# Sixteen low-bit steps of the weight conversion written for GpSimd, and a range check ordered behind the last ELU

## The chip, the cores and the metric

The kernel runs on one core of a Trainium2 chip. In this text PE is TensorE (matmuls; PEld is its weight load), DVE is VectorE, ACT is ScalarE, POOL is GpSimd, and SP is SyncE, which here only issues DMAs. The metric is the device time of one execution in microseconds. Before the change three runs gave 660.2, 660.67 and 663.14 us; their median, 660.67 us, is the time before.

## The reference, cut to what matters

The reference is a windowed attention with a few sink keys, and behind it a two-layer network with an ELU between its layers.

```python
# q, k, v: (4, 8, 768, 64) float32; n_sink = 4, window = 128
scores = q @ k^T / 8, kept where key < n_sink or 0 <= query - key < window
a = softmax(scores)
x = (a @ v), heads put side by side: 3072 tokens x 512
h = x @ w_in                        # 512 x 2048, weights arrive as float64
g = where(h > 0, h, exp(min(h, 0)) - 1)
out = (g @ w_out)                   # 2048 x 512, float32
```

The two weight matrices are products of a float32 array and a float64 scalar and reach the kernel as 64-bit words, two 32-bit words to an element.

## The kernel before, in words

The 3072 tokens are cut into nine chunks: three of 256 tokens, six of 384. For every chunk the attention is computed for four pairs of heads (scores on PE at L540/541, or L547 for the first two chunks; range reduction on DVE at L566; exponentials on ACT at L568; the probabilities are split in a high and a low 16-bit part, by ACT at L580 and DVE at L581; a transposing DMA on SP at L599 brings them into the layout of the second matmul; PE multiplies by the values at L610 and L615; ACT L623 and DVE L624 write the chunk's `x`). The feed-forward of a chunk then runs over 16 slices of the hidden width: 12 matmuls into `h` (L651), the ELU in three steps (ACT L659, DVE L661 and L662), the split of the result in `gh` (ACT L664) and `gl` (POOL L665), and 6 or 9 matmuls into the output accumulators (L672). The first two chunks are done in halves, so that only 16 of the 32 weight pieces are wanted at first.

The weights come in 32 pieces of 128 x 512 elements, piece 2f of `w_in` and 2f+1 of `w_out`. `weights(k)` makes a piece usable: a DMA of 512 KB brings the 64-bit words into `raw` (L395). Then `weight_f32` builds a 32-bit float of each: step 0 on ACT (L267) scales the high word into a PSUM tile, `acc`; step 1 on DVE (L268) takes the three top bits of the low word; step 2 on DVE (L269) takes the sign; step 3 on DVE (L270) shifts the float by three bits and puts the four together in `wv`. ACT (L416) rounds `wv` to a 16-bit `w`, and POOL (L417) writes what is left as a second 16-bit part. Steps 1 and 2 write alternating 16-bit halves of one of two buffers `wu`; six buffers `raw` hold what the DMA brought.

A planner at trace time sets the order in which each engine gets its instructions. Every piece of work is a task with an engine, an assumed duration, and the tasks it depends on; PE's order is given by positions, and for the other engines a list schedule with due times, worked backward from PE's order, decides. `keep_order` then forces that order on each engine's in-order queue. An assumed duration has no other effect than on that order.

At the end the kernel decides whether the numbers stayed in a range in which the fast path holds. `in_range` (DVE, L725 to L731, eight small operations) gathers maxima, a one-column matmul (L741) sums over partitions, `decide` (DVE L735 to L737) multiplies the verdict into a flag, and L967 writes it as an integer. All five engines load that integer (L968) and branch over the slow path (L969). In the planner's order `in_range` depends on the last exponentials (`exps_done`), not on the last DVE step of the ELU.

Of the kernel before, what the change touches and what calls it, by code (L numbers as in the profile page):

```python
# [16 lines left out]
ALU = mybir.AluOpType  # L17
# [28 lines left out]
LAG = 2  # L46
WHOLE = 2
DUP = 2
AHEAD = 5
V_AT = 7  # L50
V_AT0 = 5.0
RINGS = dict(kqs=2, kq=3, vs=2, vm=1, vhl=2, e=3, st=6, pq=3, pt=6, g=2, gh=3, x=7, wv=4, s=2, po=1, h=2, wu=2, sv=2, wps=1, raw=6)
# [40 lines left out]
class Plan:  # L93
# [7 lines left out]
    def add(self, eng, dur, fn, *args, deps=(), lat=0.0, pos=None, or_=None):  # L101

        t = Task(eng, dur, fn, args, deps, lat, pos)
        if or_:
            t.ways[or_[0]] = or_[1:]
        self.tasks.append(t)
        return t

    def ring(self, name, writers, users):

        r = self.rings.setdefault(name, [])
        r.append((writers, users))
# [128 lines left out]
def act_us(n, scaled=False):  # L241
    return 0.17 + 0.00088 * n + (0.08 if scaled else 0.0)
# [13 lines left out]

def weight_f32(nc, v, d, u, raw):

    ui = u.bitcast(U16).rearrange("p (f t) -> p f t", t=2)
    words = raw.rearrange("p (f t) -> p f t", t=2)
    halves = raw.bitcast(U16).rearrange("p (f t) -> p f t", t=4)
    return (
        lambda: nc.scalar.activation(d, words[:, :, 1].bitcast(F32), AF.Copy, scale=2.0**-111),  # L267
        lambda: nc.vector.tensor_scalar(ui[:, :, 0], halves[:, :, 1], 13, None, ALU.logical_shift_right),  # L268
        lambda: nc.vector.tensor_scalar(ui[:, :, 1], halves[:, :, 3], 0x8000, None, ALU.bitwise_and),  # L269
        lambda: nc.vector.scalar_tensor_tensor(v.bitcast(I32), d.bitcast(I32), 3, u, ALU.logical_shift_left, ALU.bitwise_or),  # L270
    )


def elu(nc, g, h, scale):
# [49 lines left out]
def fast_path(tc, ctx, first, kq, vx, wt, out, nw, flag):  # L324

    nc = tc.nc
# [63 lines left out]
    def weights(k):  # L390
        raw, v = raws[slot("raw")], wv[slot("wv")]

        def load():
            if wide:
                nc.sync.dma_start(raw, wt[k].bitcast(I32))  # L395
            else:
                nc.sync.dma_start(raw[:, :512].bitcast(F32), wt[k])

        def step(i):
            return lambda: weight_f32(nc, v, acc[2], wu[k % RINGS["wu"]], raw)[i]()  # L400

        ld = add("SP", 0.4, load, deps=[w_done.get(k - AHEAD, [None])[0]], lat=dma_us(P * 512 * 8))
        if wide:
            a = add("ACT", act_us(512), step(0), deps=[ld])
            u1 = add("DVE", 0.65, step(1), deps=[ld])
            u2 = add("DVE", 0.7, step(2), deps=[ld])
            b = add("DVE", 0.7, step(3), deps=[a, u1, u2])
            ring("wu", [u1, u2], [b])
            ring("wps", [a], [b])
            ring("raw", [ld], [a, u1, u2])  # L410
            first_acc2.append(b)
        else:
            a = b = add("ACT", act_us(512), lambda: nc.scalar.activation(v, raw[:, :512].bitcast(F32), AF.Copy, scale=W_SCALE), deps=[ld])
            ring("raw", [ld], [a])

        th = add("ACT", act_us(512), lambda: nc.scalar.activation(w[k][:, 0, :], v, AF.Copy), deps=[b])  # L416
        tl = add("POOL", 1.5, lambda: nc.gpsimd.tensor_tensor(w[k][:, 1, :], v, w[k][:, 0, :], ALU.subtract), deps=[th])  # L417
        ring("wv", [b], [tl])
        w_done[k] = th, tl

# [213 lines left out]
    def feed_forward(c, f0, f1, start):  # L634
# [4 lines left out]
        for f in range(f0, f1):  # L639
            hp = h_ps[slot("h")]  # L640
            gf = gs[slot("g")][:, :n]
            i = slot("gh")
            gh, gl = ghs[i], gls[i]

            def stage1(hp=hp, f=f):
                win = w[2 * f].rearrange("p t (a f) -> p t a f", a=ND)
                k = 0
                for d in range(ND):
                    xh, xl = x[d][:2]
                    for part, xx in ((0, xh), (1, xh), (0, xl)):  # L650
                        nc.tensor.matmul(hp[:, :n], win[:, part, d, :], xx[:, :n], start=k == 0, stop=k == 3 * ND - 1)  # L651
                        k += 1

            s1 = add("PE", 12 * (n / 2400 + 0.002), stage1, deps=[v for d in x for v in d[2:4]] + list(w_done[2 * f]), pos=start + 2 * (f - f0))
            for d in x:
                d[4].append(s1)

            sums = es_of[:, c * NF + f : c * NF + f + 1]
            a = add("ACT", act_us(n) + 0.06, lambda gf=gf, hp=hp, sums=sums: nc.scalar.activation(gf, hp[:, :n], AF.Exp, scale=1.0 / G_SCALE, accum_out=sums), deps=[s1])  # L659
            exps_done.append(a)  # L660
            b = add("DVE", 0.1 + 0.0008 * n, lambda gf=gf: nc.vector.tensor_scalar(gf, gf, -1.0, G_SCALE, ALU.add, ALU.mult), deps=[a])  # L661
            b = add("DVE", dve_us(n), lambda gf=gf, hp=hp: nc.vector.scalar_tensor_tensor(gf, gf, 0.0, hp[:, :n], ALU.min, ALU.max), deps=[b])  # L662
            ring("h", [s1], [b])
            th = add("ACT", act_us(n), lambda gf=gf, gh=gh: nc.scalar.activation(gh[:, :n], gf, AF.Copy), deps=[b])  # L664
            tl = add("POOL", pool_us(n), lambda gl=gl, gf=gf, gh=gh: nc.gpsimd.tensor_tensor(gl[:, :n], gf, gh[:, :n], ALU.subtract), deps=[th])  # L665

            def stage2(order, gl=gl, gh=gh, f=f):
                def run():
                    wout = w[2 * f + 1]
                    for k, i in order:  # L670
                        gg, part = ((gh, 0), (gh, 1), (gl, 0))[k]
                        nc.tensor.matmul(acc[i], gg[:, i * P : (i + 1) * P], wout[:, part, :], start=f == f0 and k == 0, stop=f == f1 - 1 and k == 2)  # L672
                return run

            deps = [th, tl, *w_done[2 * f + 1], *(evacs[:nt] if f == f0 else [])]
            at2 = start + 2 * (f - f0) + 1 + 2 * LAG
            if f < f1 - 1:
                s2 = [add("PE", 3 * nt * 0.215, stage2([(k, i) for k in range(3) for i in range(nt)]), deps=deps, pos=at2)]
            else:

                s2 = [add("PE", 3 * 0.215, stage2([(k, i) for k in range(3)]), deps=deps, pos=at2 + 0.01 * i) for i in range(nt)]
            ring("g", [a], [th, tl])
            ring("gh", [th], s2)
# [16 lines left out]
            saved[c, i] = sto  # L700
            evacs[i] = ev

    saved, exps_done = {}, []
    start = 0
    for c, f0, f1 in PARTS:
        if f0 == 0:
# [30 lines left out]
        nc.vector.tensor_tensor(flag, flag, some[:, 0:1], ALU.mult)  # L737

    sp = s_ps[slot("s")]
    a = add("DVE", 2.0, in_range, deps=seen + exps_done)  # L740
    b = add("PE", 0.1, lambda: nc.tensor.matmul(sp[:, 0:3], ones, some16, start=True, stop=True), deps=[a], pos=start + 2 * LAG - 1.5)  # L741
    ring("s", [b], [add("DVE", 0.6, decide, deps=[b])])
    for writer, users in later:
        writer.deps.extend(users)
# [252 lines left out]
```

## Time and profile before

| | us |
|---|---|
| median of three runs | 660.67 |
| the profiled execution | 662.14 |
| span of its instructions | 660.3 |
| PE busy | 609.9 |
| DVE busy | 458.4 |
| ACT busy | 456.9 |
| POOL busy | 338.2 |
| mean granted TensorE clock | 0.984 |

The profiled execution took 662.14 us, 1.47 us more than the median. A view by stretches gives each engine's busy time in a window; overlapping starts are counted, so an engine with no gap shows nearly the whole window. A timeline row begins with the start, in us from the start of the span, and the duration; the bracket tells how long the engine had been idle and what ended that.

### The profile page before, as it was taken

The numbers are of one execution on the slowest core, as the hardware profiler recorded it, in microseconds if no ns is written. First come the engines' busy times: TensorE is split into PE (matmuls) and PEld (weight loads), VectorE is DVE, ScalarE is ACT, GpSimd is POOL, SyncE is SP. The second block draws the span as 40 slices with busy tenths as digits, with TensorE's granted clock in tenths as the row PEclk, the third lists the DMA queues.
The fourth block names the chain that finished last, engine by engine and source line by source line (L and its number), as shares of the span: only waits on it lengthen the run. The fifth ranks groups of instructions, "written<-read, shape, count | busy, mean of one in ns | idle before, by whom it ended". The sixth has DMA issues, their size and how long they took to land.

```text
span 660.3 us, 13443 instructions
## 1 busy us (share of the span) xinstructions
PE 609.9 (92%) x4449; PEld 370.2 (56%) x4449; DVE 458.4 (69%) x1251; ACT 456.9 (69%) x1340; POOL 338.2 (51%) x497
## 2 busy tenths in 40 slices
PE   3486799789999999999999999999999999999996
PEld 2343466456776665555555556555555565555552
DVE  6999998896677776667677776758677787524222
ACT  4999786777788887767677777766677777523221
POOL 0158866785556666544555655444446564322221
PEclk9999698899999999999999999999999999999998
DMA  7989974857654586435454566555554734211001
GB/s 264 206 282 266 276 199 144 269 142 167 145 118 128 136 184 131 116 92 171 116 152 118 133 156 167 104 111 171 112 155 128 208 84 101 49 56 49 1 0 54
DMA packets 130110, 93.41 MB, mean 141 GB/s; under 512 B 104432, under 2 KB 109552, under 8 KB 130032
## 3 DMA queue, kind: packets, MB, share of 16 engines
q1 hardware_dynamic: 130032, 92.47, 53.2%
q8 instruction: 37, 0.61, 0.4%
q14 instruction: 41, 0.34, 0.2%
HBM read 59.94 MB, written 7.34 MB: 102 GB/s over the span
## 4 chain that ended last, share of the span: by engine, by line
PE 78%; DVE 7%; ACT 5%; issue 4%; POOL 3%; DMA 3%; SPq 0%; DVEq 0%; POOLq 0%; ACTq 0%
PE h L651 33%; PE acc L672 33%; PE po L610 5%; PE s L540 3%; PE s L541 3%; DMA pt<-pq 2%; PE s L547 1%; ACT e L568 1%; DVE wu L268 1%; POOL kq L487 1%; DVE wv L270 1%; DVE wu L269 1%; DVE pq L581 1%; DVE g L661 1%; POOL kq L489 1%
## 5 line engine op out<-in xcount | busy, mean ns | idle before, releaser
L651 PE MATMUL h<-x,w 128*128 128x384 f16 (+1 forms) x1728 | 276.6, 310 | 5.6 <-DVE g L662 5.6
L665 POOL TENSOR_TENSOR gl<-g,gh 128x384 f16<-128x384 f32 (+1 forms) x144 | 126.9, 882 | 215.2 <-ACT gh L664 184.4
L651 PEld LDWEIGHTS <-w 128*128 128x128 f16 x1728 | 165.6, 99 | 98.7 <-issue 5.9
L672 PE MATMUL acc<-w,gh 128*128 128x512 f16 x768 | 195.3, 384 | 0.8 <-DVE wv L693 0.8
L661 DVE TENSOR_SCALAR g<-g 128x384 f32<-128x384 f32 (+1 forms) x144 | 65.3, 454 | 115.8 <-ACT g L659 115.3
L659 ACT ACTIVATE g<-h 128x384 f32<-128x384 f32 (+1 forms) x144 | 64.9, 451 | 88.3 <-PE h L651 83.1
L581 DVE SCALAR_TENSOR_TENSOR pq<-e,st,pq 128x256 f16<-128x256 f32 (+1 forms) x192 | 107.2, 587 | 19.7 <-ACT pq L580 19.1
L672 PE MATMUL acc<-w,gl 128*128 128x512 f16 x384 | 110.6, 383 | 0.6 <-POOL gl L665 0.4
L672 PEld LDWEIGHTS <-gh 128*128 128x128 f16 x768 | 70.9, 98 | 71.5 <-issue 3.0
L568 ACT ACTIVATE e<-e,st 128x264 f32<-128x264 f32 (+1 forms) x192 | 93.4, 487 | 11.1 <-DVE st L566 9.7
L664 ACT ACTIVATE gh<-g 128x384 f16<-128x384 f32 (+1 forms) x144 | 69.3, 481 | 44.6 <-DVE g L662 44.2
L566 DVE CUSTOM_DVE_ANT_0 e<-s,m 128x264 f32<-128x264 f32 (+1 forms) x192 | 73.0, 404 | 32.1 <-PE s L541 26.8
L580 ACT ACTIVATE pq<-e,st 128x256 f16<-128x256 f32 (+1 forms) x192 | 85.1, 480 | 10.5 <-DVE st L573 10.1
L487 POOL TENSOR_TENSOR kq<-kqs,kq 128x396 fp32r<-128x396 f32 (+1 forms) x56 | 67.2, 1199 | 23.9 <-ACT kq L483 23.0
L662 DVE SCALAR_TENSOR_TENSOR g<-g,h 128x384 f32<-128x384 f32 (+1 forms) x144 | 72.6, 504 | 1.6
L672 PEld LDWEIGHTS <-gl 128*128 128x128 f16 x384 | 37.6, 99 | 47.9 <-POOL gl L665 2.5
L483 ACT ACTIVATE kq<-kqs 128x780 fp32r<-128x780 f32 (+2 forms) x56 | 48.4, 879 | 17.1 <-PE s L541 14.3
L417 POOL TENSOR_TENSOR w<-wv,w 128x512 f16<-128x512 f32 x32 | 39.5, 1236 | 38.8 <-ACT w L416 18.9
L489 POOL TENSOR_TENSOR kq<-kqs,kq 64x384 fp32r<-64x384 f32 (+1 forms) x56 | 56.7, 1013 | 4.4
L610 PE MATMUL po<-pt,vh 128*64 128x128 f16 x704 | 41.7, 230 | 17.8 <-DMA pt<-pq 7.8
L540 PE MATMUL s<-kq 128*128 128x264 f32 x160 | 56.2, 370 | 1.7 <-POOL kq L489 1.6
L610 PEld LDWEIGHTS <-vh 128*64 128x64 f16 x704 | 31.1, 115 | 29.6 <-issue 21.7
(78 smaller groups left out, 629.2 us busy)
## 6 DMA issues: line engine op xcount, KB each, us to landing
raw<-in_wt_dram SPq DMA_DIRECT2D x32, 512.0 KB, 5.6
kqs<-in_kq_dram SPq DMA_DIRECT2D x24, 456.0 KB, 3.4
kqs<-in_kq_dram SPq DMA_DIRECT2D x24, 390.0 KB, 3.3
out_dram<-wv SPq DMA_DIRECT2D x24, 256.0 KB, 2.5
vs<-in_vx_dram SPq DMA_DIRECT2D x20, 256.0 KB, 3.1
vm<-in_vx_dram SPq DMA_DIRECT2D x6, 768.0 KB, 4.6
kqs<-in_kq_dram SPq DMA_DIRECT2D x12, 326.0 KB, 4.1
vs<-in_vx_dram SPq DMA_DIRECT2D x12, 320.0 KB, 3.1
```

What stands on the lines that cost most here:

```text
L487: nc.gpsimd.tensor_tensor(buf[:, KQ_MAX : KQ_MAX + n] if c >= DUP else buf[:, kw : 2 * kw], raw[:, :n], hi[:, :n].bitcast(F32), ALU.subtract)
L540: nc.tensor.matmul(sp[:, :wd], q, hi[:, c0 : c0 + wd], start=True, stop=False)
L566: red = add("DVE", 0.13 + 0.00145 * wd, lambda ee=ee, me=me, sp=sps[e], m=m, wd=wd: nc.vector.tensor_tensor_reduce(ee, sp[:, :wd], m[:, :w ...
L568: ex = add("ACT", 0.48 + 0.00085 * wd, lambda ee=ee, me=me, rs=rs[:, e : e + 1]: nc.scalar.activation(ee, ee, AF.Exp, bias=me, scale=-1.0, ...
L580: a = add("ACT", act_us(nb * P, True), lambda src=src, hi=hi, re=re: nc.scalar.activation(hi, src, AF.Copy, scale=re), deps=[rr])
L581: b = add("DVE", dve_us(nb * P) + 0.1, lambda src=src, hi=hi, lo=lo, re=re: nc.vector.scalar_tensor_tensor(lo, src, re, hi, ALU.mult, ALU. ...
L610: nc.tensor.matmul(po[e * D : (e + 1) * D, oc], vv[:, vo : vo + D], pt[:, (2 * e + part) * nb + i, :], start=new, stop=last)
L651: nc.tensor.matmul(hp[:, :n], win[:, part, d, :], xx[:, :n], start=k == 0, stop=k == 3 * ND - 1)
L661: b = add("DVE", 0.1 + 0.0008 * n, lambda gf=gf: nc.vector.tensor_scalar(gf, gf, -1.0, G_SCALE, ALU.add, ALU.mult), deps=[a])
L662: b = add("DVE", dve_us(n), lambda gf=gf, hp=hp: nc.vector.scalar_tensor_tensor(gf, gf, 0.0, hp[:, :n], ALU.min, ALU.max), deps=[b])
L665: tl = add("POOL", pool_us(n), lambda gl=gl, gf=gf, gh=gh: nc.gpsimd.tensor_tensor(gl[:, :n], gf, gh[:, :n], ALU.subtract), deps=[th])
L672: nc.tensor.matmul(acc[i], gg[:, i * P : (i + 1) * P], wout[:, part, :], start=f == f0 and k == 0, stop=f == f1 - 1 and k == 2)
```

## The change

`weight_f32` gets a flag. For the first 16 pieces (k below `ON_POOL`) step 1 is no longer a shift on DVE but a multiply and an add on POOL: the 16-bit number times 2^-13, less 4095.5/8192, so that the conversion to an integer gives the top three bits. The planner's assumed cost of that task is 0.8 us on POOL in place of 0.65 us on DVE, and its assumed cost of the POOL step L417 goes from 1.5 to 1.22. The check's `in_range` also depends on the last step of the last ELU, and its matmul's position on PE is 1.5 later.

```diff
+ON_POOL = 16
...
-def weight_f32(nc, v, d, u, raw):
+def weight_f32(nc, v, d, u, raw, on_pool=False):
...
-    return (
+    steps = [
         lambda: nc.scalar.activation(d, words[:, :, 1].bitcast(F32), AF.Copy, scale=2.0**-111),
         lambda: nc.vector.tensor_scalar(ui[:, :, 0], halves[:, :, 1], 13, None, ALU.logical_shift_right),
         lambda: nc.vector.tensor_scalar(ui[:, :, 1], halves[:, :, 3], 0x8000, None, ALU.bitwise_and),
         lambda: nc.vector.scalar_tensor_tensor(v.bitcast(I32), d.bitcast(I32), 3, u, ALU.logical_shift_left, ALU.bitwise_or),
-    )
+    ]
+    if on_pool:
+        steps[1] = lambda: nc.gpsimd.tensor_scalar(ui[:, :, 0], halves[:, :, 1], 2.0**-13, -4095.5 / 8192, ALU.mult, ALU.add)
+    return steps
...
-            return lambda: weight_f32(nc, v, acc[2], wu[k % RINGS["wu"]], raw)[i]()
+            return lambda: weight_f32(nc, v, acc[2], wu[k % RINGS["wu"]], raw, k < ON_POOL)[i]()
...
-            u1 = add("DVE", 0.65, step(1), deps=[ld])
+            u1 = add("POOL", 0.8, step(1), deps=[ld]) if k < ON_POOL else add("DVE", 0.65, step(1), deps=[ld])
...
-        tl = add("POOL", 1.5, lambda: nc.gpsimd.tensor_tensor(w[k][:, 1, :], v, w[k][:, 0, :], ALU.subtract), deps=[th])
+        tl = add("POOL", 1.22, lambda: nc.gpsimd.tensor_tensor(w[k][:, 1, :], v, w[k][:, 0, :], ALU.subtract), deps=[th])
...
             ring("h", [s1], [b])
+            g_done.append(b)
...
-    a = add("DVE", 2.0, in_range, deps=seen + exps_done)
-    b = add("PE", 0.1, lambda: nc.tensor.matmul(sp[:, 0:3], ones, some16, start=True, stop=True), deps=[a], pos=start + 2 * LAG - 1.5)
+    a = add("DVE", 2.0, in_range, deps=seen + exps_done + g_done[-1:])
+    b = add("PE", 0.1, lambda: nc.tensor.matmul(sp[:, 0:3], ones, some16, start=True, stop=True), deps=[a], pos=start + 2 * LAG)
```

The changed file is six to seven lines longer, so its line numbers differ: the new POOL step is L276, L272 and L273 are what L269 and L270 were, L423 is L417, L704 is L697, L748 is L741, L974 to L976 are L967 to L969.

POOL at the first weights, before. Names are those of the built program with a running number: `w_132` is the first piece, `wv_120` to `wv_123` the four conversion buffers, `wu_124` and `wu_125` the two buffers of bits, `raw_126` to `raw_131` the six input buffers.

```order
L417 TENSOR_TENSOR w_132<-wv_120,w_132 128x512
L417 TENSOR_TENSOR w_133<-wv_121,w_133 128x512
L417 TENSOR_TENSOR w_134<-wv_122,w_134 128x512
L417 TENSOR_TENSOR w_135<-wv_123,w_135 128x512
L417 TENSOR_TENSOR w_136<-wv_120,w_136 128x512
L587 TENSOR_TENSOR st_96<-e_93,st_96 128x8
L590 CAST pq_102<-st_96 128x2x8
L591 TENSOR_TENSOR pq_102<-st_96,pq_102 128x8
```

POOL at the same place, changed:

```order
L276 TENSOR_SCALAR wu_124<-raw_126 128x512
L276 TENSOR_SCALAR wu_125<-raw_127 128x512
L276 TENSOR_SCALAR wu_124<-raw_128 128x512
L423 TENSOR_TENSOR w_132<-wv_120,w_132 128x512
L276 TENSOR_SCALAR wu_125<-raw_129 128x512
L423 TENSOR_TENSOR w_133<-wv_121,w_133 128x512
L276 TENSOR_SCALAR wu_124<-raw_130 128x512
L423 TENSOR_TENSOR w_134<-wv_122,w_134 128x512
L276 TENSOR_SCALAR wu_125<-raw_131 128x512
L423 TENSOR_TENSOR w_135<-wv_123,w_135 128x512
L423 TENSOR_TENSOR w_136<-wv_120,w_136 128x512
L276 TENSOR_SCALAR wu_124<-raw_126 128x512
```

The first eight of the sixteen new steps stand among the first five L423; the other eight follow among the next ones, the last of them ahead of the first split of keys (`kq`).

DVE at the first weights, before (`pq`, `st`, `e`, `s` belong to the attention of the first chunk):

```order
L573 RECIPROCAL st_96<-st_96 128x2
L269 TENSOR_SCALAR wu_125<-raw_127 128x512
L270 SCALAR_TENSOR_TENSOR wv_120<-acc_171,wu_124 128x512
L581 SCALAR_TENSOR_TENSOR pq_102<-e_93,st_96,pq_102 128x128 x2
L573 RECIPROCAL st_97<-st_97 128x2
L268 TENSOR_SCALAR wu_125<-raw_127 128x512
L269 TENSOR_SCALAR wu_124<-raw_128 128x512
L566 ISA e_92,st_98<-s_166,m_172 128x132
L566 ISA st_98 128x1
L566 ISA e_92,st_98<-s_167,m_172 128x132
L566 ISA st_98 128x1
L270 SCALAR_TENSOR_TENSOR wv_121<-acc_171,wu_125 128x512
```

DVE at the same place, changed:

```order
L579 RECIPROCAL st_96<-st_96 128x2
L273 SCALAR_TENSOR_TENSOR wv_120<-acc_171,wu_124 128x512
L587 SCALAR_TENSOR_TENSOR pq_102<-e_93,st_96,pq_102 128x128 x2
L579 RECIPROCAL st_97<-st_97 128x2
L273 SCALAR_TENSOR_TENSOR wv_121<-acc_171,wu_125 128x512
L272 TENSOR_SCALAR wu_124<-raw_128 128x512
L572 ISA e_92,st_98<-s_166,m_172 128x132
L572 ISA st_98 128x1
L572 ISA e_92,st_98<-s_167,m_172 128x132
L572 ISA st_98 128x1
L273 SCALAR_TENSOR_TENSOR wv_122<-acc_171,wu_124 128x512
L272 TENSOR_SCALAR wu_125<-raw_129 128x512
```

The L268 of pieces 0 and 1 are gone, and the third L270 (`wv_122`) has moved ahead of the attention's `pq_100`; it was behind the end of the first chunk's attention.

DVE at the end of the program, before:

```order
L731 CAST some_204<-some 128x3
L662 SCALAR_TENSOR_TENSOR g_110<-g_110,h_165 128x384
L735 TENSOR_REDUCE some<-s_166 128x1
L736 TENSOR_SCALAR some<-some 128x1
L737 TENSOR_TENSOR words<-words,some 128x1
L967 CAST words<-words 128x1
L697 TENSOR_SCALAR wv_121<-acc_169 128x512
L697 TENSOR_SCALAR wv_123<-acc_171 128x512
L968 TENSOR_LOAD words
L969 COMPARE_AND_BRANCH
```

DVE at the end, changed:

```order
L738 CAST some_204<-some 128x3
L704 TENSOR_SCALAR wv_121<-acc_169 128x512
L704 TENSOR_SCALAR wv_123<-acc_171 128x512
L742 TENSOR_REDUCE some<-s_166 128x1
L743 TENSOR_SCALAR some<-some 128x1
L744 TENSOR_TENSOR words<-words,some 128x1
L974 CAST words<-words 128x1
L975 TENSOR_LOAD words
L976 COMPARE_AND_BRANCH
```

The last ELU step (L662 before, L668 now) is ahead of `in_range` now, and the two evictions of the output (L697, now L704) are ahead of `decide`; the load of the flag and the branch follow directly on it. On PE the check's matmul, which stood ahead of the last nine accumulating matmuls, now stands behind them, and on SP the load of the flag, which stood ahead of the last three output DMAs, now stands behind them.

## Rows read from the trace of the kernel before

**Rows 1.** Busy time by stretch: the window and its length, then busy time and number of instructions of PE, PEld, DVE, ACT and POOL, the granted TensorE clock, the share of the DMA engines, and GB/s.

```profile
16.50:33.00 16.50, 7.75 (x79) 5.55 (x81) 15.48 (x50) 14.99 (x47) 3.01 (x3) 1.00 0.92 206
33.00:50.00 17.00, 14.22 (x92) 8.67 (x89) 16.24 (x53) 16.15 (x52) 9.02 (x17) 1.00 0.89 283
50.00:66.00 16.00, 10.32 (x104) 6.08 (x103) 15.96 (x35) 15.23 (x43) 13.43 (x19) 1.00 1.02 265
66.00:82.00 16.00, 11.45 (x96) 7.80 (x96) 16.00 (x34) 11.67 (x34) 12.97 (x18) 0.68 0.91 271
82.00:99.00 17.00, 16.13 (x126) 11.49 (x124) 15.74 (x41) 14.91 (x45) 11.69 (x18) 1.00 0.77 206
...
330.00:495.00 165.00, 165.00 (x1202) 97.14 (x1197) 118.94 (x322) 119.50 (x345) 85.68 (x123) 1.00 0.56 138
```

**Rows 2.** What PE waited for in the first 165 us: total, times, longest.

```profile
PE s L547 <- DVE st L566: 10.7, 10, 2.7
PE po L610 <- DMA pt<-pq: 7.8, 6, 2.5
PE po L610 <- DVE x L624: 7.7, 3, 4.1
...
PE h L651 <- DVE g L662: 5.6, 5, 2.3
```

**Rows 3.** The chain of waits between 12 and 78 us, as shares of these 66 us by line (the view cuts its line).

```profile
by line: PE h L651 11.1%; issue 10.8%; PE s L547 10.5%; ACT e L568 6.8%; DVE pq L581 6.3%; DVE wv L270 6.0%; PE po L610 5.2%; DVE wu L268 5.1%; DVE wu L269 5.1%; DVE e L566 4.3%; PE acc L672 3.9%; ACT acc L267 3.7%; DVE g L661 3.6%; ACT w L
```

**Rows 4.** Groups of instructions between 12 and 78 us: busy time and mean ns of one, and the idle time ahead.

```profile
L417 POOL TENSOR_TENSOR w<-wv,w 128x512 f16<-128x512 f32 x15 | 18.3, 1228 | 32.7 <-DVE wu L269 16.7 <-ACT w L416 14.4 <-DVE wu L268 1.6
...
L269 DVE TENSOR_SCALAR wu<-raw 128x512 uint16<-128x512 uint16 x16 | 10.7, 666 | 0.0
...
L268 DVE TENSOR_SCALAR wu<-raw 128x512 uint16<-128x512 uint16 x16 | 10.0, 625 | 0.0
```

**Rows 5.** Timeline of DVE around the first weights, and of POOL at the same time.

```profile
17.95 0.44 DVE L268 TENSOR_SCALAR wu<-raw 128x512 uint16<-128x512 uint16 x1
18.28 0.44 DVE L269 TENSOR_SCALAR wu<-raw 128x512 uint16<-128x512 uint16 x1
...
29.90 1.15 POOL L417 TENSOR_TENSOR w<-wv,w 128x512 f16<-128x512 f32 x1 [10.01 <-ACT w L416]
...
30.02 1.34 DVE L269 TENSOR_SCALAR wu<-raw 128x512 uint16<-128x512 uint16 x1
```

**Rows 6.** Timeline of DVE between 67 and 70 us, and of POOL at the same time.

```profile
66.37 3.61 POOL L417 TENSOR_TENSOR w<-wv,w 128x512 f16<-128x512 f32 x3
...
67.60 1.40 DVE L269 TENSOR_SCALAR wu<-raw 128x512 uint16<-128x512 uint16 x1
68.89 1.40 DVE L268 TENSOR_SCALAR wu<-raw 128x512 uint16<-128x512 uint16 x1
```

**Rows 7.** Groups over the whole span: two POOL operations with one input or none.

```profile
L590 POOL CAST pq<-st 128x16 f16<-128x16 f32 x64 | 16.6, 259 | 4.1
...
L364 POOL MEMSET ones<- 128x128 bf16 x1 | 0.2, 204 | 0.0
```

**Rows 8.** Timeline of PE between 66 and 78 us.

```profile
66.69 0.42 PE L610 MATMUL po<-pt,vh 128*64 128x128 f16 x4 [4.08 <-DVE x L624]
...
70.64 2.72 PE L651 MATMUL h<-x,w 128*128 128x256 f16 x12 [2.25 <-DVE g L662]
...
76.58 1.48 PE L651 MATMUL h<-x,w 128*128 128x256 f16 x12
```

**Rows 9.** Timeline of the end, all engines.

```profile
648.92 0.36 DVE L661 TENSOR_SCALAR g<-g 128x384 f32<-128x384 f32 x1 [2.94 <-ACT g L659]
...
649.19 0.32 DVE L725 TENSOR_SCALAR checks<-checks 128x144 f32<-128x144 f32 x2
...
650.47 0.55 DVE L662 SCALAR_TENSOR_TENSOR g<-g,h 128x384 f32<-128x384 f32 x1
...
651.71 0.91 POOL L665 TENSOR_TENSOR gl<-g,gh 128x384 f16<-128x384 f32 x1 [4.13 <-issue]
...
651.96 0.59 PE L672 MATMUL acc<-w,gh 128*128 128x512 f16 x2
...
652.16 0.16 DVE L735 TENSOR_REDUCE some<-s 128x1 f32<-128x3 f32 x1 [1.14 <-PE s L741]
...
652.67 0.39 PE L672 MATMUL acc<-w,gl 128*128 128x512 f16 x1
...
652.74 0.15 DVE L967 CAST words<-words 128x1 int32<-128x1 f32 x1
...
654.40 0.69 DVE L697 TENSOR_SCALAR wv<-acc 128x512 f32<-128x512 f32 x1 [0.60 <-PE acc L672]
```

**Rows 10.** Timeline of SP's queue at the end: the last three output DMAs.

```profile
653.82 1.63 SPq L698 DMA_DIRECT2D out_dram<-wv  x3
```

**Rows 11.** The load of the flag and the branch: duration as minimum, median and maximum, then first and last start.

```profile
L968 SPq TENSOR_LOAD <-words x1: 471/471/471, 652.9 to 652.9; - x1
...
L969 DVEq COMPARE_BRANCH  x1: 72/72/72, 655.3 to 655.3; - x1
L969 SPq COMPARE_BRANCH  x1: 53/53/53, 655.5 to 655.5; - x1
...
L969 DVEq EVENT_SEMAPHORE  x1: 21/21/21, 658.8 to 658.8; - x1
```

More of the change, by code (lines that the diff above doesn't have):

```diff
@@ L701, in feed_forward @@
             evacs[i] = ev
-    saved, exps_done = {}, []
+    saved, exps_done, g_done = {}, [], []
     start = 0
```

## The prediction

> **What bounds the kernel now.** I read the view by stretches first. From 330 us on PE is busy for 165.00 of 165 us [rows 1]: nothing that the change does on DVE or POOL can shorten that part, and it lies behind it. In the five stretches from 16.5 to 99 us PE is busy for 59.9 of 82.5 us, so it idles for 22.6; DVE is busy for 79.4 (96%), ACT for 73.0 (88%), POOL for 50.1 (61%), and the DMA engines for 77 to 102% [rows 1]. This is the only place where the conversion can pay. The waits of PE, read second, say the same: before 165 us it waits longest for DVE steps (10.7 for the score's reduction, 7.7 for `x`, 5.6 for the ELU), but also 7.8 for transposing DMAs [rows 2]. Third, the chain of waits from 12 to 78 us: L268 holds 5.1% of 66 us, 3.4 us, about as much as L269 and L270, and the rest alternates between PE, ACT and DVE [rows 3]. So DVE is the tightest engine there, with ACT right behind.
>
> **The moved step.** The sixteen L268 all lie between 12 and 78 us and are busy for 10.0 us, 625 ns each [rows 4]. One that nothing disturbs takes 0.44, and the next DVE instruction starts 0.33 after it [rows 5]; 16 x 0.44 = 7.0, so 3.0 of the 10.0 are waiting. Not all of the 10.0 is on the way to the end: the chain passes through 3.4 [rows 3]. That is my gain on DVE, 3.4 us. ACT's cover can cap it: ACT idles for only 1.5 + 0.8 + 0.8 = 3.1 us from 16.5 to 66 us [rows 1], but 1.3 of the 3.4 belong to the one L268 at 68.89 [rows 6], so 2.1 must fit into 3.1 and do.
>
> On POOL the new step is a two-byte, strided, one-input operation that the trace does not have. Its bounds: a CAST of 16 elements takes 0.26 us [rows 7], and hardly less than this can be paid for 512; L417, with the same 512 elements but two inputs, takes 1.15 undisturbed [rows 5] and 1.23 on average [rows 4]. A MEMSET of 128 elements takes 0.20 [rows 7], four times that is 0.8. I take 0.8, which is nearer to L417, the row with the same count. So 16 x 0.8 = 12.8 us are added to POOL, 4.2 by the lower bound and 19.7 by the upper. The place for it: the first steps fall where POOL idles for 13.5 of 16.5 us; from 33 to 66 us POOL is busy for 22.5 of 33 [rows 1], and the order puts some ten steps there, so 30.5 of 33, as tight as ACT with 31.4. POOL has room, but no slack is left; DVE's L270 now waits for POOL's step, and behind it in DVE's queue stand the attention's reductions.
>
> The trace shows what POOL does to DVE: an L269 that starts at 30.02, when an L417 has run since 29.90, takes 1.34 instead of 0.44 and ends 0.3 behind the L417; at 67.60 and 68.89 L269 and L268 take 1.40 each under three L417 in a row [rows 5, 6]. The sixteen L269 stay on DVE and take 10.7 [rows 4], 3.7 more than 7.0. That came with 38.4 us of POOL work between 16.5 and 82 us [rows 1]; 12.8 more, in proportion, adds 1.2, and as a third of L269's time is on the chain (3.4 of 10.7), 0.4 of it. With the other DVE operations of this kind I take 0.6. The bounds are 0 and the whole 12.8, if every POOL step held DVE for its full length.
>
> The Trainium skill speaks against the change here: SBUF — State Buffer, § SBUF: two separate sides, says that VectorE and GpSimd have one port pair in common, which is an exclusive lock: whichever starts first has it for its whole instruction, and the other blocks. The rows agree. By the row's proportion the loss is 0.6; by the rule taken at its worst it is what the third rival below prices.
>
> For the step's own price GPSIMD Engine Reference, § 3.1, gives 769 ns for a tight one-input loop over 512 elements; by it the sixteen would take 12.3 us as an estimate, and the sum above would not change.
>
> The order also moves DMAs: on SP one 512 KB load of weights goes ahead of a load of keys and two transposes near 20 us, and the conversion of piece 2 goes ahead of the first chunk's attention. I cost this at nothing, since the weights that come early are not loaded later; its cover is gone if the transposes, for which PE waits 7.8 us [rows 2], come later by it. ACT's loads are the same in number. L417's smaller assumed cost has only its part in the order.
>
> So the first 100 us give 3.4 - 0.6 = 2.8 us.
>
> **The range check.** Now the last L661 ends at 649.28, eight small operations run from 649.19 on, and the last L662 starts at 650.47 [rows 9]. Behind the change L662 starts at about 649.3, 1.15 earlier. Then `gl`, which starts at 651.71 and ends at 652.62, ends at 651.5, and the matmul that waits for it until 652.67 can start right behind the two of 651.96, at a pace of 0.59 - 0.39 = 0.20, at 652.37: 0.3 us are gained on PE. The last eviction on DVE moves from 654.40 to 654.10 and ends at 654.8.
>
> But that is not what ends the program. Today the flag's integer is written at 652.74 to 652.89, and its load, 0.47 us, lies beside the last matmuls. SP issues its output DMAs 0.92 after the load began (653.82 against 652.90), the last until 655.45; DVE branches at 655.3, SP at 655.5 [rows 9 to 11]. From DVE's branch to its next instruction at 658.8 pass 3.4 us [rows 11]; the end is 660.3. Behind the change the four operations from L735 to L967, 0.73 us (652.16 to 652.89), follow the last eviction: 654.72 to 655.45. Then the load, 0.47, and the branch: DVE at 656.0, SP at 655.45 + 0.92 = 656.4. That is 0.7 and 0.9 later than before. I take 0.8 us lost, the 0.3 won already in it. The bounds: 1.2, if SP's load starts later than DVE's write; a gain of 0.3, if what follows the branch no longer competes with the output DMAs and is shorter by the 0.9 and more.
>
> **The sum.** 662.14 - 2.8 + 0.8 = 660.1 us for the profiled execution; less 1.47, as the median of the runs lies below the profiled one, 658.7 us.
>
> **Rivals.** *The clock stays up.* PE's granted clock is 0.68 from 66 to 82 us [rows 1]; PE had idled for 4.08 us ahead of 66.69, waiting for `x` on DVE, and the twelve L651 at 70.64 take 2.72 us, at 76.58 only 1.48 [rows 8]. If DVE comes early enough, that wait shrinks to less than the other waits and the engine stays at 2.4 instead of 1.2 GHz. The slow twelve L651 and the six L672 behind them would give back about 1.25 each, 2.5 us. Then 662.14 - 3.4 - 2.5 + 0.8 - 1.47 = 655.6. For it: the wait is on DVE, ahead of which fourteen of the sixteen L268 stand. [...]
>
> *Hidden anyway.* ACT at 95% from 33 to 66 us and the DMA engines at 89 to 102% hold the pace [rows 1], and the chain passes to them where L268 leaves it. Only the end counts: 662.14 + 0.8 - 1.47 = 661.5. For it, the transposes in the list of waits; against it, the 3.4 us on the chain.
>
> *Slower: POOL holds DVE.* The new steps run where POOL is 95% busy; each holds up a DVE instruction, by the lock or because L270 waits for it. An average hold of half a step, 0.4, on an engine that is 96% busy, is 16 x 0.4 = 6.4 us, against 3.4 won. Then 662.14 - 3.4 + 6.4 + 0.8 - 1.47 = 664.5. It decides from a hold of 0.2 us per step on. For it: L268 itself loses 0.2 each today (3.0 in 16) where POOL was less full. Against it: eight of the sixteen steps run early, and the step is no longer in DVE's own queue.
>
> **How the numbers follow.** The forecast has 40%, with a range of its own from 657 to 660.3; the clock 27%, 652 to 657.4; hidden anyway 15%, 660.3 to 663; POOL holds DVE 18%, 662 to 668. A measurement of this kernel tells no change from 0.5%, 3.3 us, either way: faster is below 657.4, slower above 664.0. Faster: the clock's 27% and 7 of the forecast's, 34%. Slower: 12 of POOL's 18%. The same: 54%. The range, leaving out a tenth at either end, is 653.5 to 664.
>
> **What would show it.** Sixteen POOL steps of about 0.8 us; L268 with 16 left; DVE below 90% from 16.5 to 66 us and ACT above 95%. L269's mean near 0.7 and not near 1.0. The last L662 at 0.4 behind the last L661; DVE's L735 behind the last eviction, and both branches 0.7 to 0.9 later behind the last matmul than now. The prediction is wrong if the granted clock from 66 to 82 us is near 1.00, if L270 waits for POOL for more than 3 us in all, if POOL's step takes over 1.1 us, or if the end from the last matmul on is no longer than now.

## The result, and the profile after

The changed kernel is slower. Eight runs of it have a median of 667.78 us (665.53 to 668.41), eight of the kernel before 662.32 us (660.2 to 664.76). The two medians lie 5.5 us apart; the ratio on record, which is not the quotient of the medians, is 1.0065, with a 95% interval from 1.0047 to 1.0083, which is 4.3 us. Forecast were 658.7 us and a range up to 664.0; the three runs of before known then had a median of 660.67, and by the ratio this would become 665.0. Its profiled execution took 665.97 us, with a span of 663.8 (before: 662.14 and 660.3).

The same stretches as [rows 1], with a last line that sums the first five, and one more stretch, 120 to 140 us, the last line for before:

```profile
16.50:33.00 16.50, 6.98 (x66) 5.06 (x66) 14.20 (x45) 14.18 (x45) 4.81 (x6) 1.00 0.73 201
33.00:50.00 17.00, 13.65 (x94) 8.37 (x90) 15.84 (x50) 14.71 (x46) 13.42 (x20) 1.00 0.89 255
50.00:66.00 16.00, 12.26 (x114) 7.71 (x112) 13.55 (x30) 12.73 (x36) 11.74 (x19) 0.89 0.84 243
66.00:82.00 16.00, 8.60 (x67) 4.78 (x65) 11.84 (x28) 12.49 (x36) 14.11 (x20) 0.92 0.78 198
82.00:99.00 17.00, 16.33 (x123) 11.27 (x124) 13.92 (x33) 14.00 (x41) 12.16 (x18) 0.88 0.75 229
sum 82.50, PE 57.82 PEld 37.19 DVE 69.35 ACT 68.11 POOL 56.23; mean PE 11.56 PEld 7.44 DVE 13.87 ACT 13.62 POOL 11.25
...
120.00:140.00 20.00, 12.57 (x95) 8.15 (x94) 17.98 (x31) 14.17 (x36) 14.30 (x15) 0.83 0.64 215
```

```profile
120.00:140.00 20.00, 15.95 (x116) 9.87 (x115) 17.28 (x37) 15.57 (x42) 15.35 (x16) 0.91 0.65 208
```

DVE is relieved, from 79.4 to 69.4 us of 82.5. But ACT did not fill up behind it: it fell from 73.0 to 68.1, the DMA share fell too, and PE got 57.8 us instead of 59.9. POOL alone is busier, 56.2 us in place of 50.1. When an engine is unloaded and ACT, PE and the DMA engines get less busy as well, they wait longer for each other. The low clock has moved rather than gone: 0.92 from 66 to 82 us in place of 0.68, but 0.89, 0.88 and 0.83 in stretches that had 1.00, 1.00 and 0.91.

The chain from 12 to 78 us, as [rows 3], and what PE waited for up to 165 us, as [rows 2]:

```profile
by line: DMA raw<-in_wt_dram 15.3%; DVE pq L587 9.6%; PE h L657 9.1%; issue 8.8%; ACT e L574 5.7%; PE s L553 5.3%; ACT pq L586 4.9%; DMA pt<-pq 4.7%; POOL wu L276 3.9%; DVE wv L273 3.9%; POOL w L423 3.6%; PE po L616 3.6%; DVE e L572 3.5%; D
```

```profile
PE s L553 <- DVE st L572: 10.5, 8, 4.8
PE s L553 <- DMA kqs<-in_kq_dram: 6.2, 1, 6.2
PE h L657 <- DVE g L668: 4.9, 4, 2.1
PE po L616 <- DMA pt<-pq: 4.7, 2, 4.4
PE po L616 <- DVE x L630: 4.5, 2, 2.8
PE s L546 <- DVE st L572: 3.1, 1, 3.1
```

The loads of the weights, which had no share among those that [rows 3] shows (the last is 3.6%), now hold 15.3% of 66 us; the new step holds 3.9%, where the DVE step that it replaced held 5.1%. DVE, which before lists no wait for the loads between 10 and 100 us, now has this one:

```profile
DVE wu L272 <- DMA raw<-in_wt_dram: 4.8, 4, 2.4
```

The new step itself, all sixteen:

```profile
L276 POOL TENSOR_SCALAR wu<-raw x16: 762/844/1147, 9.2 to 71.3; 128x512 uint16<-128x512 uint16 x16
...
its engine sat idle before it (us, times) until:
  DMA raw<-in_wt_dram: 12.8, 5
  DVE wv L273: 7.7, 2
who waited for it (us, times):
  DVE e L572: 0.8, 1
  DVE wv L273: 0.6, 1
```

It takes 0.84 us, 0.8 was assumed, and DVE waits for it for only 1.4 us in all. What stands out is the other direction: POOL waits 12.8 us for weights to arrive, 7.1 of them ahead of the very first piece, and 7.7 for DVE to give a buffer back.

At the end of the program (timeline of DVE, then the branch, first and last start, as in [rows 9, 11]; last, PE's branch before; PEldq is PE's sequencer):

```profile
656.28 0.69 DVE L704 TENSOR_SCALAR wv<-acc 128x512 f32<-128x512 f32 x1 [0.60 <-PE s L748]
656.89 0.15 DVE L742 TENSOR_REDUCE some<-s 128x1 f32<-128x3 f32 x1
...
657.46 0.15 DVE L974 CAST words<-words 128x1 int32<-128x1 f32 x1
```

```profile
L976 SPq EVENT_SEMAPHORE  x8: 17/17/17, 661.8 to 662.4; - x8
...
L976 PEldq COMPARE_BRANCH  x1: 4244/4244/4244, 658.5 to 658.5; - x1
L976 DVEq COMPARE_BRANCH  x1: 72/72/72, 658.5 to 658.5; - x1
...
L976 DVEq EVENT_SEMAPHORE  x1: 21/21/21, 661.7 to 661.7; - x1
L976 PEldq EVENT_SEMAPHORE  x1: 51/51/51, 662.8 to 662.8; - x1
```

```profile
L969 PEldq COMPARE_BRANCH  x1: 3944/3944/3944, 653.5 to 653.5; - x1
...
L969 PEldq EVENT_SEMAPHORE  x1: 51/51/51, 657.5 to 657.5; - x1
```

PE's branch takes 4.24 us. Before, it began at 653.5, beside the last matmuls, took 3.94 and was over at 657.5, ahead of DVE's next instruction at 658.8 [rows 11]. Now it begins behind the flag, at 658.5, and PE comes out of it last of the five engines, at 662.8, some 0.4 us behind SP; the span ends at 663.8.

### The profile page after: what moved, and what is told of

Its sections match the earlier page's. It is cut to its first block, busy times and chain, and to the rows that moved or that the text cites. A ratio compares the mean times of both kernels' runs of the same rounds, so it can differ in the third digit from the quotient of the medians.

```text
span 663.8 us, 13443 instructions
## 1 busy us (share of the span) xinstructions
PE 609.6 (92%) x4449; PEld 370.2 (56%) x4449; DVE 455.7 (69%) x1235; ACT 456.5 (69%) x1340; POOL 351.5 (53%) x513
## 4 chain that ended last, share of the span: by engine, by line
PE 79%; DVE 6%; ACT 4%; POOL 4%; DMA 3%; issue 2%; SPq 0%; DVEq 0%; POOLq 0%; ACTq 0%
PE acc L679 34%; PE h L657 34%; PE po L616 5%; PE s L546 3%; PE s L547 2%; DMA raw<-in_wt_dram 2%; DVE pq L587 1%; DMA pt<-pq 1%; ACT e L574 1%; POOL kq L493 1%; POOL kq L495 1%; DVE g L667 1%; DVE wv L273 1%; ACT pq L586 1%; PE s L553 1%
## 5 line engine op out<-in xcount | busy, mean ns | idle before, releaser
L668 DVE SCALAR_TENSOR_TENSOR g<-g,h 128x384 f32<-128x384 f32 (+1 forms) x144 | 72.7, 505 | 1.7
L495 POOL TENSOR_TENSOR kq<-kqs,kq 64x384 fp32r<-64x384 f32 (+1 forms) x56 | 55.1, 983 | 4.4
L423 POOL TENSOR_TENSOR w<-wv,w 128x512 f16<-128x512 f32 x32 | 39.8, 1249 | 18.6 <-ACT w L422 17.8
```

## The experiments

Theory P was that POOL's step itself costs the time (it holds DVE up or comes late), theory O that the planner's new order does. All ratios are to the kernel before on the same chip.

**The edits one by one.** The range check alone:

```diff
-ON_POOL = 16
+ON_POOL = 0
-        tl = add("POOL", 1.22, ...
+        tl = add("POOL", 1.5, ...
```

> Only the range check is moved; the weights are as before. Theory (the flag is the last thing that the program waits for, and PE's branch of some 4 us follows on it): 1.3 to 1.6 us slower than before, ratio 1.002; the last L657 to L679 part of PE 0.3 us shorter, from the last accumulating matmul to the end 7.9 us in place of 6.3. Rival (the end of the program varies by that much anyway, the loss lies all in the weights): ratio 1.000.

Measured: 1.0008 (0.999 to 1.0026), 0.5 us: less than the 1.3 to 1.6 expected, though the interval excludes neither these nor nothing. In its profile 8.18 us pass from the start of the last accumulating matmul to the end. That time needs more than one profile: it is 6.29 to 7.72, 7.10 on average, in eleven profiles with the check as before (before's own is the shortest of all), and 7.82 to 8.18, 7.99 on average, in seven with the check moved. So the move costs 0.9 us there, less the 0.3 that PE gains: from the last ELU's exponential to the last of these matmuls 5.36 us pass in the changed kernel, 5.68 before.

The weights alone (POOL step and assumed cost, range check as before):

```diff
-    a = add("DVE", 2.0, in_range, deps=seen + exps_done + g_done[-1:])
+    a = add("DVE", 2.0, in_range, deps=seen + exps_done)
...
-..., deps=[a], pos=start + 2 * LAG)
+..., deps=[a], pos=start + 2 * LAG - 1.5)
```

> The range check is as before; the POOL step and the assumed cost of 1.22 us are kept. Theory (two thirds of the loss lie in the first 165 us): 2.2 to 3.5 us slower than before, ratio 1.004, with the last accumulating matmul 2.2 us later. Rival (the check makes all of the loss, the head moves by chance of one profile): ratio 1.000.

Measured: 1.0056 (1.003 to 1.0081). With 1.0008 for the check this is the whole loss. Now the two edits in the weights apart, the POOL step with the old assumed cost (1.5) and the assumed cost of 1.22 with no POOL step:

> The POOL step alone: range check and the assumed cost of L423 (1.5 us) as before. Theory P (the step itself holds up DVE and its buffers, wherever the rest stands): as the weights alone, 2 to 3.5 us slower, ratio 1.003 to 1.005. Theory O (the loss is the order that the smaller assumed cost brings): no slower than before, 655 to 661 us.

> No POOL step, range check as before; only the assumed cost of L423 in the planner is 1.22 in place of 1.5 us, so every instruction is the same and only the order differs. Theory P: within 1 us of before. Theory O: 2 to 3.5 us slower than before.

Measured: the step alone 1.0021 (1.0003 to 1.004; its median is only 0.4 us above that of its runs of before), the assumed cost alone 1.0131 (1.01 to 1.0162), 8.7 us, with not one instruction added or removed. Both theories missed a size: the step costs less than P said, the number in the planner more than O said. The two do not add up (0.21% and 1.31% against 0.56% together); each edit makes its own order.

**Engine and order apart.** The planner can be told one thing and the instruction be issued on another engine at that place. So the step was put on POOL in the order of before, and on DVE in the new order; and, to take its length away in either order, it was cut to one column of 512, which leaves out the low bits of the others.

```diff
 # order of before, step on POOL: the planner still assumes DVE
-            u1 = add("POOL", 0.8, step(1), deps=[ld]) if k < ON_POOL else add("DVE", 0.65, step(1), deps=[ld])
+            u1 = add("DVE", 0.65, step(1), deps=[ld])
...
 # new order, step on DVE
-        steps[1] = lambda: nc.gpsimd.tensor_scalar(ui[:, :, 0], halves[:, :, 1], 2.0**-13, ...
+        pass
...
 # one column
-        steps[1] = lambda: nc.gpsimd.tensor_scalar(ui[:, :, 0], halves[:, :, 1], ...
+        steps[1] = lambda: nc.gpsimd.tensor_scalar(ui[:, 0:1, 0], halves[:, 0:1, 1], ...
```

> The order of before (PE, ACT, DVE and SP get their instructions as before, the planner assumes the step on DVE), but the sixteen steps are issued on POOL at the places where L268 stood; range check as before. Theory O (the loss is the new order, the step itself gains what DVE is relieved of): 1 to 3 us faster than before, ratio 0.995 to 0.9985. Theory P (POOL's step holds DVE up or comes too late, in any order): 1.5 to 3.5 us slower, ratio 1.002 to 1.005.

> The order of the changed kernel, range check included, but the sixteen steps are issued on DVE as shifts, at the places where POOL's steps stood in time. Theory O: as slow as the changed kernel or slower, ratio to before 1.006 to 1.013. Theory P: only the check's 0.001 and a little of the order is left, ratio 1.000 to 1.003.

> The order of before, but the L268 of the first sixteen pieces treats one column of 512 (the other low bits are left out: zeros written once at the start by POOL). This is DVE relieved, with nothing given to POOL. My prediction's term (3.4 us of L268 on the way to the end): 2.1 to 3.4 us faster, ratio 0.995 to 0.997. Rival (ACT and the DMAs set the pace, hidden anyway): within 1 us of before.

> The changed kernel in its own order, but POOL's sixteen steps treat one column of 512 (low bits left out as in the run before). Theory P: the time that POOL's step costs goes, 3 us or more under the changed kernel, ratio to before 1.002 or less. Theory O: the order alone is left, within 1.5 us of the changed kernel, ratio to before 1.004 to 1.0065.

> The order of before with the sixteen steps on POOL, but each treats one column of 512 (the other low bits are left out). Theory Q (the step is late because POOL's queue in front of it waits, whatever its length): DVE still waits 5 us or more for L276, ratio to before 1.003 to 1.006. Theory D (its length of 0.82 us is what DVE waits for): DVE waits under 2 us for L276, ratio 0.9985 to 1.001, as the run with the short step on DVE (0.9985).

| step of the first 16 pieces | order of before | new order (check moved too) |
|---|---|---|
| on DVE, 512 columns | 1 (before) | 1.0068 (1.0043 to 1.0093) |
| on POOL, 512 columns | 1.0059 (1.0037 to 1.008) | 1.0065 (the changed kernel) |
| on DVE, one column | 0.9985 (0.9967 to 1.0002) | |
| on POOL, one column | 0.9969 (0.9953 to 0.9985) | 1.0041 (1.0018 to 1.0064) |

Read down the left column: all of the relief of DVE, with next to nothing given to POOL, is worth 1.0 to 2.1 us (the first of the two is not told from nothing); the step's length on POOL then costs 6.0 us (1.0059 less 0.9969). Read across: the new order costs 4.8 us where the step has one column (1.0041 less 0.9969), 0.5 of it the check's. Read the right column: in that order it makes no difference that can be seen whether DVE or POOL does the step, and its length costs 1.6 us, less than two intervals tell from nothing. So P holds in the old order, O in the new one, and the changed kernel, which has the new one, loses by O.

What an order costs can come in two ways: PE waits longer, or it runs at the lower of its two clocks for longer. These are the busy times of the whole span with one column, in the old order (span 662.2 us) and in the new one (664.4):

```profile
PE 611.6 (92%) x4449; PEld 371.5 (56%) x4449; DVE 450.5 (68%) x1235; ACT 456.8 (69%) x1340; POOL 341.2 (52%) x515
```

```profile
PE 614.7 (93%) x4449; PEld 372.6 (56%) x4449; DVE 453.5 (68%) x1235; ACT 456.5 (69%) x1340; POOL 343.1 (52%) x515
```

PE idles for no longer in the new order, 49.7 us against 50.6, but is busy for 3.1 us more with the same matmuls, at a granted clock of 0.973 against 0.984. Over all runs of these two the mean clock is 0.978 and 0.987. Among the 154 runs of the changed versions, a run whose clock is 0.01 lower than its version's mean is about 3 us longer, so by estimate some 3 of the 4.8 us come with the clock. In the profiles of the changed kernel and of before, both at 0.984, it is the other way: PE is busy for 609.6 and 609.9 us and idles for 54.2 and 50.4. No run holds the clock fixed, so the two ways stay unseparated.

Why the relief is worth so little is seen in the sums of busy time over 16.5 to 99 us (before 79.4 on DVE, 73.0 on ACT) and in DVE's waits from 10 to 100 us, before and then in the run with one column on DVE (its lines after 370 count two more than the changed kernel's):

```profile
sum 82.50, PE 62.34 PEld 40.16 DVE 72.22 ACT 72.60 POOL 49.99; mean PE 12.47 PEld 8.03 DVE 14.44 ACT 14.52 POOL 10.00
```

```profile
DVE e L566 <- PE s L547: 1.5, 4, 0.8
...
DVE g L661 <- ACT g L659: 0.6, 2, 0.4
```

```profile
DVE e L574 <- PE s L555: 3.6, 5, 1.6
DVE g L669 <- ACT g L667: 2.4, 3, 1.5
DVE wv L273 <- ACT acc L270: 2.3, 4, 1.1
```

DVE has 7.2 us less to do and waits for PE and ACT instead; ACT's busy time hardly changes, 72.6 us in place of 73.0. And with the step on POOL in the old order, DVE's wait for it and ACT's for DVE, with 512 columns and then with one:

```profile
DVE wv L273 <- POOL wu L276: 10.2, 6, 3.4
...
ACT acc L270 <- DVE wv L273: 5.7, 5, 2.9
...
ACT w L422 <- DVE wv L273: 3.1, 2, 2.4
```

```profile
DVE wv L273 <- POOL wu L276: 6.3, 5, 2.0
...
ACT acc L270 <- DVE wv L273: 2.6, 3, 1.7
ACT w L424 <- DVE wv L273: 2.5, 2, 1.8
```

The run with one column met neither expectation whole. DVE still waits 6.3 us for it, as theory Q said, though one such step takes only 0.19 us; but the time is that of theory D and better: these 6.3 us cost nothing that can be seen, and the likely reason is that they lie in the time that DVE was given. With its whole length DVE waits 3.9 us more, ACT's waits for L273 go from 5.1 to 8.8 us, and the end comes 6.0 us later.

**What in the order costs.** First the assumed cost of L423, at 1.4 and at 1.6, in a kernel with the instructions of before:

> Instructions as before, only the assumed cost of L423 in the planner is 1.4 in place of 1.5 us. Theory L (the order that the planner finds is a draw: each small change of a cost gives another one, with no direction): ratio anywhere from 0.995 to 1.015, not on the line from 1.0 (at 1.5) to 1.0131 (at 1.22). Rival (the smaller the cost the later what POOL owes to others is placed): on that line, 1.004 to 1.006.

> As the run before, with an assumed cost of 1.6 us; only some 40 rows of DVE's, ACT's and POOL's queues and 20 of SP's stand elsewhere than before. Theory L: within 0.5% of before, either sign. Rival (a line through 1.5 and 1.22): 0.995 to 0.997.

Measured: 1.0059 (1.0041 to 1.0078) and 1.0028 (1.001 to 1.0047). At 1.4 this is on the rival's line; at 1.6 it is not, and there theory L, within 0.5% of either sign, held. Of the four values 1.22, 1.4, 1.5 and 1.6 the fastest is 1.5, though L423 takes 1.23 us [rows 4]. A truer number gave a slower order. Not settled by this is whether the order of 1.5 is a lucky one or the cost stands for something that the planner does not count.

Then SP's queue. The slow order of 1.22 with SP's DMAs in the order of before (`two_orders` takes one engine's queue from another plan):

```diff
-    tasks = plan.order()
+    tasks = two_orders(plan, old, ('SP',))
```

> The slow order of the run with the assumed cost alone (1.22 us, no POOL step, range check as before) on PE, DVE, ACT and POOL, but SP issues its DMAs in the order of before. Theory S (what the new order loses is in SP's queue: loads of weights stand behind transposing DMAs that wait for DVE): at least half of the 1.0131 goes, ratio to before 1.006 or less. Rival (it is the order on DVE, ACT and POOL): ratio stays at 1.010 to 1.015.

Measured: 1.0208 (1.0181 to 1.0235), slower than 1.0131 and outside both expectations. The theory falls for this order. From 12 to 100 us the loads held 14.9% of the chain and the transposing DMAs 9.2% in the run with the assumed cost alone; with SP's old order the loads are not among the shares shown and the transposes hold 19.5%. So one kind of DMA took the other's place in the chain. In the order of the changed kernel SP's queue was not exchanged. Next the two buffers `wu`, for which POOL waits 7.7 us:

```diff
-    wu = rows("wu", [P, 512], I32)
+    wu = rows("wu", [P, 512], I32, 4)
```

> The changed kernel in its own order, but four buffers wu in place of two, so that POOL's step of piece k waits for L273 of piece k-4 and not k-2 (POOL waits for L273 for 7.7 us before its steps in the changed kernel). Theory W (the ring of two makes the step late and DVE wait): 1.5 us or more under the changed kernel, ratio to before 1.004 or less. Rival (it is the loads of the weights and the order of DVE and SP): as the changed kernel, 1.005 to 1.008.

Measured: 1.0064 (1.0043 to 1.0084); the rival. The wait is gone from POOL's list, and POOL waits for ACT ahead of L423 instead, 17.6 us in place of 10.7. Then one misplaced instruction. In DVE's new order one reduction of a pair of scores stands twelve instructions behind its twin, behind the conversion of pieces 16 and on, and PE waits for it (timeline of DVE; PE's waits from 120 to 150 us, both of the changed kernel):

```profile
129.03 0.42 DVE L572 CUSTOM_DVE_ANT_0 e<-s,m 128x264 f32<-128x264 f32 x1
...
138.27 0.41 DVE L572 CUSTOM_DVE_ANT_0 e<-s,m 128x264 f32<-128x264 f32 x1
```

```profile
PE po L616 <- DMA pt<-pq: 4.4, 1, 4.4
PE s L546 <- DVE st L572: 3.1, 1, 3.1
PE h L657 <- DVE g L668: 1.4, 1, 1.4
```

```diff
+    for r0, r1 in twins:
+        between = [t for t in tasks[tasks.index(r0) + 1 : tasks.index(r1)] if t.eng == "DVE"]
+        if len(between) > 8:
+            ...
+            tasks.remove(r1)
+            tasks.insert(max(tasks.index(r0), ready) + 1, r1)
```

> The changed kernel with one DVE instruction moved: the reduction L572 of the second score at 138.27 us goes back directly behind its twin at 129.03. Theory R (this misplaced reduction is a part of what the new order loses): the wait of PE of 3.06 us goes and 1.5 to 3 us of it reach the end, ratio to before 1.002 to 1.0045. Rival (the wait only moves on, to the next transposing DMA or the next ELU step): as the changed kernel, 1.0055 to 1.0075.

> As the run before, and the second reduction at 81.36 us also moved beside its twin at 77.31. Theory R: under the run before by up to 1 us, ratio to before 1.001 to 1.0045. Rival: as the changed kernel, 1.0055 to 1.0075.

Measured: 1.0056 (1.0034 to 1.0077) and 1.0048 (1.0031 to 1.0065). The same view of the first of them (the ELU's last step is L669 here):

```profile
PE po L617 <- DMA pt<-pq: 4.4, 1, 4.4
PE h L658 <- DVE g L669: 4.1, 2, 2.8
```

The wait of 3.1 us is gone, and the ELU step on the same engine waits in its place, 4.1 instead of 1.4. The rival held for the first run; for the second its 1.0048 lies between the two, and a small gain is not excluded.

One thing in the order that the runs show was not tested. The pieces from 16 on keep their shift on DVE. Between 78 and 200 us these sixteen shifts took (groups by line, before and changed; the second number is the mean in ns):

```profile
L268 DVE TENSOR_SCALAR wu<-raw 128x512 uint16<-128x512 uint16 x16 | 10.9, 682 | 0.0
```

```profile
L271 DVE TENSOR_SCALAR wu<-raw 128x512 uint16<-128x512 uint16 x16 | 14.0, 882 | 0.0
```

The instruction is the same and its mean goes from 0.68 to 0.88 us. It is 0.66 to 0.74 in all six versions with the order of before in the weights, and 0.82 to 0.94 in all seven with the changed kernel's order. In both traces every one of them that lasts over 0.55 us begins while a POOL instruction runs. So the new order puts more of them beside POOL; how much of the 3.1 us reaches the end, no run shows.

Last, the version that the runs pointed to, the order of before with POOL's step for the first six pieces alone, where POOL idles:

```diff
-ON_POOL = 16
+ON_POOL = 6
```

> The order of before, and only the first six pieces take POOL's step (POOL is idle there for most of the time); the other ten stay shifts on DVE. Theory (the loss comes from the ten later steps, where POOL has a queue): 0.9985 to 1.001, the version most likely to beat both. Rival (every POOL step costs, a quarter of a microsecond each): 1.002 to 1.003.

Measured: 1.001 (0.9996 to 1.0024). This lies at the upper end of the theory's range. These six cost nothing that can be told, and bring nothing; the changed kernel is beaten, the one before is not. No run found a version faster than before that also does the whole work.

## Why the prediction was wrong

The forecast was a sum of 3.4 us won on DVE, 0.6 lost to POOL, 0.8 lost at the end, and nothing for the order. Along the table the runs put these at 2.1 won (old order, one column on POOL), 1.6 lost for the step's length in the new order, 0.5 lost at the end, and 4.3 lost for the order, 4.3 in all. The term set at nothing is the largest.

- *"That is my gain on DVE, 3.4 us."* Measured are 1.0 to 2.1 us (0.9985, whose interval reaches 1.0002, and 0.9969). The share of a line in the chain of waits [rows 3] was taken for what its removal gives. The text did test it against ACT's idle time, 3.1 us, and found room; the run with one column shows that ACT used none of it: its busy time from 16.5 to 99 us is 72.6 us there, 73.0 before.
- *"With the other DVE operations of this kind I take 0.6."* The place was wrong, and by the order the size. Where the loss was looked for, DVE's sign step did not suffer: L272 takes 0.69 us on average between 12 and 78 us, 0.67 before [rows 4], though POOL is busy for 6.1 us more from 16.5 to 99 us. Behind 78 us the shifts that stayed on DVE did, 0.88 us in place of 0.68; a hold of DVE beside POOL is therefore not ruled out as part of what the order costs. (The lock has a condition that the prediction left out: the Trainium skill, SBUF — State Buffer, § SBUF: two separate sides, gives it for VectorE operations in a 2-port mode or with two SBUF inputs. No run here tests the condition.) In the order of before the step's length costs 6.0 us through DVE's wait for it; in the new order 1.6, not told from nothing.
- *"I cost this at nothing"*, of the moved DMAs, and *"L417's smaller assumed cost has only its part in the order"*. This is the step that failed and that turned the sign: with one column on POOL, where next to nothing of the step is left, the new order takes the time from 0.9969 to 1.0041, 4.8 us, of which the check is 0.5. With the whole POOL step in place, the assumed cost of 1.22 instead of 1.5 goes from 1.0021 to 1.0056, 2.3 us; alone it costs 8.7. The excerpts of the order that were read ahead of the prediction were those of the first weights and of the end; what the order moved in between was not looked at.
- *The range check* was right in sign and size: 0.8 us were forecast, 0.9 less 0.3 is read from the profiles, and 0.5 measured, within -0.7 and 1.7. Missed was that all five loads of the flag now start together: DVE's branch is at 658.5, 2.6 us behind the start of the last accumulating matmul, where it was 1.3, so 1.3 later and not 0.7. The text followed DVE and SP; in the changed kernel PE, whose branch takes 4.2 us, comes out last, by 0.4 us. The Trainium skill bears on this: Runtime: NRT & Kernel Launch, § Instruction fetch mechanics, says that a taken branch to code outside the prefetched pages waits for a fetch. The trace agrees on PE, whose branch takes 4.24 us, and on DVE, whose branch of 72 ns is followed by 3.2 us without an instruction, but not on POOL, whose next instruction starts 0.2 us behind its branch. That a fetch is the cause, no run shows.
- *The cases.* Of the four the third rival, POOL holds DVE, came nearest: 664.5 us, 3.8 above the 660.67 from which it started, where 4.3 were measured. It had 18%, and the nearness is in part luck: its mechanism, DVE held by the POOL step, is seen only in the order of before, where DVE waits for it for 10.2 us in six places; in the changed kernel DVE waits 1.4. Of the eight steps that were to run early, five ran before 33 us. Of the forecast's own signs, DVE below 90% was right (43.6 of 49.5 us from 16.5 to 66) and ACT above 95% was wrong (41.6 of 49.5, 84%), which says that DVE's relief did not reach ACT. Of the four signs that were to prove the prediction wrong, three did not come (L273 waits 0.6 us for POOL, the step's median is 0.84 us, the end is longer), and the clock from 66 to 82 us came half way, to 0.92, while it fell elsewhere. None of the four looked at the order.

By edits, then: 1.4 us for the step with its own order, 2.3 for the assumed cost on top of it, and about 0.6 for the check give the 4.3. What stays open is which rows of the new order cost its 4 us. The `wu` ring and the late reductions explain no more than a part that the runs cannot tell from nothing; SP's queue was exchanged only in another order and made that one slower; the lower clock and the longer shifts beside POOL go with the new order but were not taken apart from it.

## What to carry to other kernels

Where a list scheduler sets the order, a cost in its table is an edit of the program: run it alone before it travels with another change, because here it cost 2.3 to 8.7 us and the step that it came with 1.4, and a number nearer to the trace was no better. A line's share of the chain of waits is not its worth: here 3.4 us on the chain were worth 1.0 to 2.1. Cut the line to one column at the same place in the order and the run tells what its removal can bring, before anybody looks for another engine to do it. A wait that is removed is worth something only if the next one is not just as late. And an order also decides which instructions run side by side: compare the mean time of instructions that nobody touched.

## What the runs showed of the hardware

A shift of 128x512 16-bit numbers on DVE takes 0.44 to 0.45 us where no POOL instruction runs at its start, and up to 1.43 where one does. The branch at the end is recorded with 3.9 to 4.2 us on PE's sequencer and with 45 to 72 ns on the other four. The flag's load takes 0.46 to 0.48 us on four engines before (three of them start at once, DVE's later one takes 0.81), and 0.72 to 0.80 us on all five in the changed kernel, where all start within 0.1 us. And from the last matmul to the end the same instructions take 6.3 to 7.7 us from one profile to another, so a difference of 1 us there is not read from two profiles.
